# Turning the down-projection of a gated feed-forward block: seven transposed products per pair of f tiles

## The chip, the cores and the metric

The kernel runs on one core of a Trainium2 chip. The metric is the device time in microseconds (us). "TensorE" or PE is the matrix engine, DVE the vector engine, ACT the scalar engine, POOL is GpSimd, and SP is the engine that issues nearly all DMAs here.

## What is computed

One transformer block with adaptive layer norm on 2048 rows of 512 elements: attention with 32 query heads and 8 key-value heads over the last 512 cached positions, and a gated feed-forward block of width 1792, both in float32.

```python
mod = (silu(c) @ w_mod).reshape(c.shape[0], 6, 1, -1)
sa, ca, ga, sb, cb, gb = (mod[:, i] for i in range(6))
h = layernorm(x) * (1 + ca) + sa
x = x + ga * attention(h, k_cache, v_cache, wq, wo)
h = layernorm(x) * (1 + cb) + sb
x = x + gb * ((gelu(h @ w_gate) * (h @ w_up)) @ w_down)
```

## The kernel before

**Numbers.** Every float32 operand of a matmul is kept as two float16 tiles, a high and a low part, and a product is three matmuls (`mm3`): high by high, high by low, low by high. ACT or POOL makes a high part, DVE or POOL the low part by subtraction.

**Stages.** Attention runs first, in 512 steps (`T`) whose order on all engines is written out by hand. In its second half, from step `T // 2 + 30` on, the feed-forward weights are scaled, split and stored to DRAM (`prep_set` for gate and up, `prep_wd` for down), mostly on POOL; the products of the first gate and up sets end attention's last steps. Then comes the feed-forward part. There only SP's queue keeps its written order; on the other engines a planner in the compiler orders the instructions, by written order as priority and by assumed durations.

**The feed-forward part.** The 2048 rows are done in two halves of 1024 (two blocks of 512 columns of the transposed activations). In each half the 14 f tiles of 128 are taken in 7 pairs, so there are 14 pair steps `n`; `n % 7` is the pair, `n // 7` the half. A pair step has two sets, `q = 2n` (gate) and `q = 2n + 1` (up), 28 in all. A set is a 2x2 block product done as seven products instead of eight (the scheme with combined operands t1 to t4 and s1 to s4, `PROD`, `CHAIN`), in the order `ORDER = (1, 2, 6, 7, 5, 4, 3)`; each of the seven steps has 6 matmuls of 512 columns. Partial sums are read in the middle of a chain: the copies after products 1, 6 and 7 are the parts that later sums share. Gate results go through gelu into `G`; up results are multiplied in, and the product is split into parts `A[n, key]`, with key "11", "21" (first block of rows; f tile 1, 2) and "12", "22" (second block).

**Down-projection before.** For each pair step there are 8 row tiles of 128 rows. For each, `y_tasks` multiplies the two parts `A` (as the stationary operand) by the down weights (256 rows, 512 columns, moving): two products of three matmuls into a bank `py`, which one DVE operation adds to the row's sum `acc` with a scale. The tasks are queued in `nexty` at the end of set `2n + 1`, and `y_next` takes one after steps 1, 2, 5 and 6 of each set. `acc` has 8 buffers, for the 8 row tiles of a half: they hold the first half's rows of the residual when the feed-forward part starts. At the last pair of a half `f_final` writes the tile to the output and loads the second half's row tile.

**Names that the change touches.** `prep_wd` (weights, with the gate vector of `rows[5]` multiplied into the columns), `d_spread` (its scales), `result` in `f_items` (parts of the product), `place` (where a copy lies), `f_final`, `attn_final` (which loaded the first half's sums), `y_next` and the loop over `q`, `put_off(n, fn)` (does `fn` after `n` further calls of `tick`, one per step).

Of the kernel before, what the change touches and what calls it, by code (L numbers as in the profile page):

```python
# [9 lines left out]

F32 = mybir.dt.float32
F16 = mybir.dt.float16
BF16 = mybir.dt.bfloat16
AF = mybir.ActivationFunctionType
ALU = mybir.AluOpType
# [23 lines left out]
GU = 2.0 ** -38  # L39
PRE = 2.0 ** -20  # L40
TINY = 1e-36
NOT = 10
LDGAP = 1
NRAW = 5
NRW = 2
GW = 3
NACC = 5
NP16 = 4
# [13 lines left out]
def block_kernel(ctx: ExitStack, tc: tile.TileContext, x, kT, v, wq, wo, wg, wu, wd, cT, wc, wm, out):  # L62
# [14 lines left out]
    def pair(tag, name, bufs):  # L77
        return pool.tile([P, 2, 512], F16, tag=tag, name=name, bufs=bufs)

# [89 lines left out]

    for name, n in (("kmax", HKV), ("kinv", HKV), ("vmax", HKV), ("vsc", HKV), ("wsc", HQ // 2), ("qsc", HQ // 2),  # L170
                    ("ksc", HQ // 2), ("osc", HKV), ("ysc", HKV), ("fsc", NF), ("finv", NF), ("gsc", NF // 2),
                    ("dsc", NF // 2), ("dysc", NF // 2), ("ma", 1), ("mf", 1), ("gam", 2)):
        stats(name, n)

    def col(name, i=0):
        return ST[name][:, i:i + 1]
# [58 lines left out]
    def pool_ts(out, src, a, b=1.0, op0=ALU.mult, op1=ALU.mult):  # L235
        nc.gpsimd.tensor_scalar(out, src, a, b, op0=op0, op1=op1)
# [39 lines left out]
    def o_spread(qd, m, more):  # L276
# [10 lines left out]

        then(second)

    def f_spread(i, m):  # L290
        w = little("lw", 1, 2)
        norm2(w, m, 2, 1.0 / TOP13)
        pool_ts(col("finv", i), w, col("mf"))
        then(lambda: nc.vector.reciprocal(col("fsc", i), w))
        if i % 2 == 0:
            g = col("gsc", i // 2)
            pool_ts(g, col("finv", i), 1.0 / GU)
            then(lambda: nc.vector.reciprocal(g, g))

    def d_spread(n, m, more):  # L300
        w, t = little("lw", 1, 2), little("lt", 1, 2)
        norm2(w, m, 2, 1.0)
        pool_ts(w, w, col("gam", 1), 1.0 / TOP14)
        pool_ts(w, w, 1e-30, 1.0, ALU.max)
        pool_ts(t, col("finv", 2 * n), 2.0 ** 19, col("finv", 2 * n + 1))
        pool_ts(col("dysc", n), t, 2.0 ** 19, w)

        def second():
            nc.vector.reciprocal(col("dsc", n), w)
            more()  # L310

        then(second)
# [289 lines left out]
    def get_wo():  # L602
        return pair("wo", "wo", 8)
# [118 lines left out]
    def at(key, *fns):  # L722
        later.setdefault(key, []).extend(fns)
# [225 lines left out]
    def attn_final(ti):  # L949
        y1[ti] = dram.tile([P, D], F32, name=f"y{ti}")  # L950
        dma(y1[ti], acc[ti])
        nxt = (ti + 2 * QT) % NT
        if ti < 2 * QT:
            own, steps = ln_tile(2, ti, lambda: acc[ti])
# [301 lines left out]
    def f_items(q, hold=None):  # L1256
        n, m = divmod(q, 2)
        st = {}
        done = set()

        def add(k, src):
            nc.vector.tensor_tensor(st[k], st[k], st[src], op=ALU.add)

        def gelu(key, src):

            def apply():
                dst = tmp("fg") if key == "21" else src
                nc.scalar.activation(dst, src, AF.Gelu_apprx_tanh, scale=col("finv", f_scale(q)))
                G[n, key] = dst

            return (apply,)

        def result(key, src):
            if m == 0:
                for step in gelu(key, src):
                    step()
            else:
                g = G.pop((n, key))
                nc.vector.scalar_tensor_tensor(g, g, col("gsc", n % NP), src, op0=ALU.mult, op1=ALU.mult)  # L1279
                t = pair("ot", "at", NOT)  # L1280
                nc.scalar.activation(t[:, 0, :], g, AF.Copy)  # L1281
                nc.vector.tensor_tensor(t[:, 1, :], g, t[:, 0, :], op=ALU.subtract)
# [83 lines left out]

    def prep_wd(n, b):
        m, st = {}, {}
        outs = [staged() for _ in range(2)]

        def load(k):
            st[k] = raw("raw")
            dma(st[k], wd[(2 * n + k) * P:(2 * n + k + 1) * P, :])

        def stat(k):
            if not m:
                m["m"] = little("lm", 4, dtype=BF16)
            sumsq(m["m"][:, k:k + 1], st[k])

        def more():  # L1380
            m["g"] = pool.tile([P, D], F32, tag="gs", name="gs", bufs=1)
            pool_ts(m["g"], rows[5], col("dsc", n))

        def spread():
            d_spread(n, m["m"], more)

        def make(k):
            nc.gpsimd.tensor_tensor(st[k], st[k], m["g"], op=ALU.mult)
            halves(outs[k][0]["t"], st[k])

        sched(b, (lambda: load(0), [lambda: stat(0), nop]), b + 7)
        sched(b + 1, (lambda: load(1), [lambda: stat(1), spread, nop]), b + 4, b + 9)
        for k in range(2):
            sched(b + 7 + 2 * k, (outs[k][1], [lambda k=k: make(k), lambda k=k: store(("wd", n, k), outs[k][0]["t"], 0)]), b + 10 + 2 * k)

    at(T // 2 + 34, lambda: mod_row(5))
    for n in range(NP):
# [1 line left out]
        prep_set(2 * n, b)  # L1399
        prep_set(2 * n + 1, b + 13)  # L1400
        prep_wd(n, b + 21)
    for k in range(2):
        at(T - 1 + 2 * k, lambda k=k: WO.update({("f", 0, k): fetch(("wd", 0, k), get_wo())}))
# [4 lines left out]
    pending = {"raw": [], "rw": []}  # L1408
    loads.sort(key=lambda l: l[0])
    released = {"raw": [0] * NRAW, "rw": [0] * NRW}  # L1410
    for pos, (load, steps), kind, ahead in loads:
        assert len(pos) == len(steps), (pos, len(steps))
        go = pos[0] - ahead
# [140 lines left out]
        at(("f", q, k), *fns)  # L1554

    for n in range(1, 2 * NP):
        for k in range(2):
            f_at(2 * n + 1, 2 * k, lambda n=n, k=k: WO.update({("f", n, k): fetch(("wd", n % NP, k), get_wo())}))
    for q in range(3, NQ):
        for k, at_ in ((0, 2), (3, 2), (1, 3), (2, 4)):  # L1560
            f_at(q - 1, at_, lambda q=q, k=k: set_fetch(("f", q), ("f", q % (2 * NP)), k))
# [18 lines left out]
                step(q + 2 * off, fn)  # L1580

    def f_final(ti):
        if ti >= 2 * QT:
            dma(rows_of(out, ti), acc[ti])
        else:
            put_off(2, lambda: dma(rows_of(out, ti), acc[ti]))
            put_off(5, lambda: load_acc(ti + 2 * QT, y1[ti + 2 * QT]))

    f_done = {(0, k) for k in ORDER} | {(1, 1), (1, 2), (1, 6)}
    for q in range(NQ):  # L1590
        n, m = divmod(q, 2)
        its = items(NG + q) if q < 2 else f_items(q)
        for k, pk in enumerate(ORDER):
            if (q, pk) not in f_done:
                all_of(its[pk])
            run(("f", q, k))
            tick()
            if k in ((1, 2, 5, 6) if q < NQ - 1 else (1, 5)):
# [45 lines left out]
```

## Time and profile before

| | |
|---|---|
| median of 3 runs | 1746.63 us (1746.54 to 1746.77) |
| the profiled execution | 1747.24 us |
| its span, first to last instruction | 1745.3 us |
| TensorE busy | 1723.9 us, 99% of the span, 8080 matmuls |
| DVE, ACT, POOL busy | 79%, 70%, 52% |
| granted TensorE clock | 1.000 |

The span is a little shorter than the execution's time, which also holds what lies before the first and after the last instruction. A row of a group reads: line, engine, operation, output and input tiles, shapes, count, then busy time and the mean of one in ns, then the engine's idle time just before these instructions and what ended it. Rows of the timeline give the start and the duration in us. The duration of a single matmul in such a row contains the pipeline's depth; matmuls start one behind the other at a shorter distance.

### The profile page before, as it was taken

To read this page: it belongs to the slowest core of one execution; us is meant where nothing else is said; L and a number is where in the kernel's file an instruction comes from. 1 tells how busy PE (TensorE), PEld (TensorE's weight loads), DVE (VectorE), ACT (ScalarE), POOL (GpSimd) and SP (SyncE) were. 2 spreads that over 40 slices of the span, in tenths; PEclk is the share of its full clock that TensorE was granted. 3 is DMA by queue.
4 is the path that set the end of the run, shared out by engine and by line. 5 is a ranking of instruction groups with operands and counts; after the bars stand their busy time and mean duration, and the time that the engine had idled before them with its cause. 6 is when DMAs were issued, how large, how long until landed. Compare 5 with 4: busy or idle time off the path is not lost.

```text
span 1745.3 us, 25819 instructions
## 1 busy us (share of the span) xinstructions
PE 1723.9 (99%) x8080; PEld 793.2 (45%) x8082; DVE 1380.3 (79%) x2404; ACT 1213.7 (70%) x2751; POOL 901.1 (52%) x1120
## 2 busy tenths in 40 slices
PE   7999999999999999999999999999999999999999
PEld 5444444444444444444444444444444444444444
DVE  7898898888889999888888888888886655555555
ACT  6988788888879777888777777877784544323232
POOL 4889778776788884654475565554521224000000
PEclk9999999999999999999999999999999999999999
DMA  7999999999999999999999999999986753252222
GB/s 234 219 206 211 211 215 206 225 209 219 213 219 228 212 205 183 212 208 235 212 201 215 203 220 199 211 214 213 195 184 145 205 174 117 81 183 77 88 75 76
DMA packets 667498, 329.71 MB, mean 189 GB/s; under 512 B 561504, under 2 KB 580192, under 8 KB 667360
## 3 DMA queue, kind: packets, MB, share of 16 engines
q1 hardware_dynamic: 667072, 327.54, 82.0%
q8 instruction: 64, 1.05, 0.3%
q14 instruction: 74, 0.61, 0.1%
q10 hardware_dynamic: 288, 0.52, 0.1%
HBM read 131.73 MB, written 59.90 MB: 110 GB/s over the span
## 4 chain that ended last, share of the span: by engine, by line
PE 87%; DVE 4%; ACT 4%; issue 1%; DMA 1%; POOL 1%; SPq 0%; ACTq 0%; POOLq 0%; DVEq 0%
PE py L87 25%; PE po L87 17%; PE ps L87 16%; PE fa L87 8%; PE qa L87 8%; PE fc L87 4%; PE qc L87 4%; PE qb L87 2%; PE fb L87 2%; ACT ee L983 1%; DVE p L1000 1%; ACT p L995 1%; DVE nm L974 1%; DMA pt<-p 1%; PE pq L87 1%
## 5 line engine op out<-in xcount | busy, mean ns | idle before, releaser
L983 ACT ACTIVATE ee<-ps,nm 128x512 f32<-128x512 f32 x512 | 350.2, 684 | 199.2 <-DVE nm L974 196.5
L1000 DVE SCALAR_TENSOR_TENSOR p<-ee,rr,p 128x512 f16<-128x512 f32 x512 | 460.7, 900 | 5.1 <-ACT p L995 4.7
L974 DVE TENSOR_REDUCE nm<-ps 128x1 f32<-128x512 f32 x512 | 350.3, 684 | 111.5 <-PE ps L87 108.4
L87 PE MATMUL ps<-k,qt 128*128 128x512 f16 x1536 | 414.9, 379 | 5.4 <-ACT ee L983 4.2
L87 PE MATMUL po<-pt,v 128*128 128x512 f16 x1536 | 373.0, 379 | 2.0 <-DMA pt<-p 2.0
L995 ACT ACTIVATE p<-ee,rr 128x512 f16<-128x512 f32 x512 | 364.4, 712 | 13.1 <-DVE rr L991 8.8
L87 PE MATMUL py<-wo,ot 128*128 128x512 f16 x1536 | 371.5, 379 | 0.0
L87 PEld LDWEIGHTS <-w 128*128 128x128 f16 x2184 | 213.5, 98 | 258.1 <-DVE w L1045 0.6
L87 PEld LDWEIGHTS <-v 128*128 128x128 f16 x1536 | 149.9, 98 | 184.3 <-DMA pt<-p 2.5
L87 PEld LDWEIGHTS <-ot 128*128 128x128 f16 x1536 | 150.2, 98 | 181.7 <-DVE ot L731 0.5
L87 PEld LDWEIGHTS <-qt 128*128 128x128 f16 x1536 | 145.9, 98 | 176.7 <-issue 4.3
L87 PE MATMUL py<-wo,at 128*128 128x512 f16 x672 | 160.5, 379 | 0.0
L943 DVE SCALAR_TENSOR_TENSOR acc<-py,dysc,acc 128x512 f32<-128x512 f32 x112 | 81.5, 747 | 51.1 <-PE py L87 51.1
L731 DVE SCALAR_TENSOR_TENSOR ot<-po,ot 128x512 f16<-128x512 f32 x128 | 87.7, 685 | 33.0 <-ACT ot L730 32.2
L87 PEld LDWEIGHTS <-at 128*128 128x128 f16 x672 | 65.7, 98 | 79.3
L983 ACT ACTIVATION_READ_ACCUMULATOR ee<-ps,nm 128x1 f32 x512 | 99.9, 195 | 0.0
L943 DVE SCALAR_TENSOR_TENSOR acc<-py,ysc,acc 128x512 f32<-128x512 f32 x128 | 94.7, 740 | 6.2 <-PE py L87 6.2
L1281 ACT ACTIVATE at<-fg 128x512 f16<-128x512 f32 x56 | 35.2, 628 | 72.2 <-DVE fg L1279 71.9
L87 PE MATMUL qa<-t,w 128*128 128x512 f16 x348 | 84.9, 379 | 0.0
L87 PE MATMUL fa<-t,w 128*128 128x512 f16 x336 | 82.0, 379 | 0.0
L730 ACT ACTIVATE ot<-po 128x512 f16<-128x512 f32 x128 | 73.9, 577 | 5.0 <-PE po L87 5.0
L232 POOL TENSOR_TENSOR lw<-lw,half__86 128x1 f32<-128x1 f32 x37 | 22.1, 598 | 104.6 <-DVE lw L182 104.5
(222 smaller groups left out, 2379.9 us busy)
## 6 DMA issues: line engine op xcount, KB each, us to landing
w<-kept SPq DMA_DIRECT2D x123, 256.0 KB, 3.2
wo<-kept SPq DMA_DIRECT2D x60, 256.0 KB, 3.8
raw<-in_wo SPq DMA_DIRECT2D x56, 256.0 KB, 3.3
kept<-stage SPq DMA_DIRECT2D x56, 256.0 KB, 3.4
kept<-w SPq DMA_DIRECT2D x39, 256.0 KB, 3.4
rw<-in_wq SPq DMA_DIRECT2D x38, 256.0 KB, 3.2
hs<-hf SPq DMA_DIRECT2D x32, 256.0 KB, 2.9
pt<-p SPq DMA_TRANSPOSE x512, 3.5
```

The source lines that it names most:

```text
L87: nc.tensor.matmul(ps, a, b, start=first and n == 0, stop=last and n == 2, skip_group_check=chain)
L232: nc.gpsimd.tensor_tensor(out, out, half_, op=ALU.pow)
L730: nc.scalar.activation(t[:, 0, :], src, AF.Copy, scale=scale)
L731: return lambda: nc.vector.scalar_tensor_tensor(t[:, 1, :], src, scale, t[:, 0, :], op0=ALU.mult, op1=ALU.subtract)
L943: nc.vector.scalar_tensor_tensor(acc[ti], st["p"], by, acc[ti], op0=ALU.mult, op1=ALU.add)
L974: nc.vector.tensor_reduce(nm, E[t]["ps"], axis=AX.X, op=ALU.max, negate=True)
L983: nc.scalar.activation(e, E[t]["ps"], AF.Exp, bias=E[t]["nm"], scale=1.0, accum_out=sm[:, t % 2:t % 2 + 1])
L995: nc.scalar.activation(p16[:, 0, :], E[t]["e"], AF.Copy, scale=E[t]["r"])
L1000: nc.vector.scalar_tensor_tensor(p16[:, 1, :], E[t]["e"], E[t]["r"], p16[:, 0, :], op0=ALU.mult, op1=ALU.subtract)
L1281: nc.scalar.activation(t[:, 0, :], g, AF.Copy)
```

## The change

For six of the seven pairs (`turned(n)`), in both halves, the down-projection is computed transposed: the weights become the stationary operand and the 512 columns of a block the moving one, and the 2x2 block product (two f tiles by two halves of the 512 output columns, two blocks of rows) is done by the same scheme of seven products, once for each of two groups of 128 columns in a half (`yt_tasks`). For that:

- `prep_wd` stores four weight tiles per pair instead of two: the plain and combined blocks. The gate vector is no longer multiplied into the columns; it is now a factor per partition (`dyc`) that DVE applies when it adds a product to the sum.
- `result` keeps the four products of a pair until the last is there; `sums_of` makes the combinations t1, t3, t2, t4 by four subtractions on POOL, and their parts on ACT (high) and POOL (low). Plain parts are made of "11", "21" and "22" only.
- Each product's bank is read by DVE at once (`yt_add`) and added to one of eight transposed sums `yt`, of 128 columns by 512 rows, which use the buffers of `acc`.
- After the sixth pair the sums are turned back: ACT parts the 16-bit halves of the float32 words into two blocks (`split`), a transposing DMA turns them (`turn`), ACT puts the halves together again as rows (`yt_rows`), and POOL adds them to the row tile, which is loaded from DRAM when `yt` gives its buffer free. The seventh pair is done as before, on the row tiles; whichever of the two additions comes second calls the output (`f_final`).
- The fourteen tasks are taken one per step of the sets, the last ones two per step. Four weight tiles are fetched per pair.
- More buffers for parts (`NOT`), own buffers for the down weights' loads (`wr`), one gate copy in the buffers of `k`, a smaller scratch area for descriptors.

```diff
-NOT = 10
+NOT = 12
 LDGAP = 1
 NRAW = 5
 NRW = 2
+NWR = 2
...
+    def turned(n):
+
+        return n % NP < NP - 1
...
-        pool_ts(w, w, col("gam", 1), 1.0 / TOP14)
+        pool_ts(w, w, 1.0 if turned(n) else col("gam", 1), 1.0 / TOP14)
         pool_ts(w, w, 1e-30, 1.0, ALU.max)
         pool_ts(t, col("finv", 2 * n), 2.0 ** 19, col("finv", 2 * n + 1))
         pool_ts(col("dysc", n), t, 2.0 ** 19, w)
+        if turned(n):
+            pool_ts(ST["dyc"][:, KT * n:KT * (n + 1)], cols[:, 5, :], col("dysc", n))
...
-            at(now[0] + 3, lambda: load_acc(nxt, y1[nxt]))
...
-                g = G.pop((n, key))
+                g = G[n, key]
                 nc.vector.scalar_tensor_tensor(g, g, col("gsc", n % NP), src, op0=ALU.mult, op1=ALU.mult)
-                t = pair("ot", "at", NOT)
-                nc.scalar.activation(t[:, 0, :], g, AF.Copy)
-                nc.vector.tensor_tensor(t[:, 1, :], g, t[:, 0, :], op=ALU.subtract)
-                A[n, key] = t
+                if not turned(n):
+                    parts(key, G.pop((n, key)), nc.vector)
+                elif key != "12":
+                    parts(key, g, nc.vector)
+                else:
+                    sums_of()
+
+        def parts(key, g, eng):
+            t = A[n, key] = pair("ot", "at", NOT)
+            nc.scalar.activation(t[:, 0, :], g, AF.Copy)
+            eng.tensor_tensor(t[:, 1, :], g, t[:, 0, :], op=ALU.subtract)
+
+        def sums_of():
+            g = {k: G.pop((n, k)) for k in ("11", "12", "21", "22")}
+            for o, a, b in (("11", "12", "11"), ("12", "22", "12"), ("22", "22", "11"), ("21", "21", "22")):
+                nc.gpsimd.tensor_tensor(g[o], g[a], g[b], op=ALU.subtract)
+                parts({"11": "t1", "12": "t3", "22": "t2", "21": "t4"}[o], g[o], nc.gpsimd)
...
-                return tmp("fg")
+                return pool.tile([P, QB], F32, tag="k", name="fg", bufs=2) if k == 6 else tmp("fg")
...
-        outs = [staged() for _ in range(2)]
+        outs = [staged() for _ in range(4)]
+        l, r = slice(0, 256), slice(256, 512)
 
         def load(k):
-            st[k] = raw("raw")
+            st[k] = pool.tile([P, D], F32, tag="wr", name="wr", bufs=NWR)
             dma(st[k], wd[(2 * n + k) * P:(2 * n + k + 1) * P, :])
 
         def stat(k):
...
             sumsq(m["m"][:, k:k + 1], st[k])
 
         def more():
-            m["g"] = pool.tile([P, D], F32, tag="gs", name="gs", bufs=1)
-            pool_ts(m["g"], rows[5], col("dsc", n))
+            if not turned(n):
+                m["g"] = pool.tile([P, D], F32, tag="gs", name="gs", bufs=1)
+                pool_ts(m["g"], rows[5], col("dsc", n))
 
         def spread():
             d_spread(n, m["m"], more)
...
             nc.gpsimd.tensor_tensor(st[k], st[k], m["g"], op=ALU.mult)
             halves(outs[k][0]["t"], st[k])
 
-        sched(b, (lambda: load(0), [lambda: stat(0), nop]), b + 7)
-        sched(b + 1, (lambda: load(1), [lambda: stat(1), spread, nop]), b + 4, b + 9)
-        for k in range(2):
-            sched(b + 7 + 2 * k, (outs[k][1], [lambda k=k: make(k), lambda k=k: store(("wd", n, k), outs[k][0]["t"], 0)]), b + 10 + 2 * k)
+        def out(k):
+            return outs[k][0]["t"] if k < 3 else outs[k][0]["t"][:, :, l]
+
+        def keep_it(k):
+            return lambda: store(("wd", n, k), out(k), 0)
+
+        def tt(o, a, c, op):
+            nc.gpsimd.tensor_tensor(o, a, c, op=op)
+
+        def d0():
+            times(st[0], col("dsc", n))
+            times(st[1], col("dsc", n))
+            halves(out(0)[:, :, l], st[0][:, l])
+            halves(out(0)[:, :, r], st[1][:, l])
+
+        def d1():
+            halves(out(3), st[1][:, r])
+            tt(st[1][:, r], st[0][:, r], st[1][:, r], ALU.add)
+            tt(st[0][:, r], st[0][:, l], st[0][:, r], ALU.subtract)
+
+        def d2():
+            tt(st[0][:, l], st[1][:, r], st[0][:, l], ALU.subtract)
+            tt(st[1][:, l], st[1][:, l], st[0][:, l], ALU.subtract)
+
+        if not turned(n):
+            sched(b, (lambda: load(0), [lambda: stat(0), nop]), b + 7, kind="wr")
+            sched(b + 1, (lambda: load(1), [lambda: stat(1), spread, nop]), b + 4, b + 9, kind="wr")
+            for k in range(2):
+                sched(b + 7 + 2 * k, (outs[k][1], [lambda k=k: make(k), keep_it(k)]), b + 10 + 2 * k)
+            return
+        sched(b, (lambda: load(0), [lambda: stat(0), nop]), b + 10, kind="wr")
+        sched(b + 1, (lambda: load(1), [lambda: stat(1), spread, d2, nop]), b + 4, b + 9, b + 11, kind="wr")
+        sched(b + 7, (outs[0][1], [d0, keep_it(0)]), b + 10)
+        sched(b + 8, (outs[3][1], [d1, keep_it(3)]), b + 11)
+        sched(b + 10, (outs[1][1], [lambda: halves(out(1), st[0]), keep_it(1)]), b + 13)
+        sched(b + 11, (outs[2][1], [lambda: halves(out(2), st[1]), keep_it(2)]), b + 14)
...
+    def wd_fetch(n, k):
+        t = get_wo()
+        WO["f", n, k] = fetch(("wd", n % NP, k), t if k < 3 else t[:, :, 0:256])
+
+    for k, pos in zip((0, 3, 2, 1), (T - 1, T + 1, T + 3, T + 6)):
+        at(pos, lambda k=k: wd_fetch(0, k))
...
-        for k in range(2):
-            f_at(2 * n + 1, 2 * k, lambda n=n, k=k: WO.update({("f", n, k): fetch(("wd", n % NP, k), get_wo())}))
+        for k, at_ in ((0, 1), (2, 3), (1, 4), (3, 5)) if turned(n) else ((0, 1), (1, 4)):
+            f_at(2 * n + 1, at_, lambda n=n, k=k: wd_fetch(n, k))
...
+        assert ti in back
+        if ti not in halfway:
+            return halfway.add(ti)
         if ti >= 2 * QT:
             dma(rows_of(out, ti), acc[ti])
         else:
             put_off(2, lambda: dma(rows_of(out, ti), acc[ti]))
-            put_off(5, lambda: load_acc(ti + 2 * QT, y1[ti + 2 * QT]))
+
+    YT, YR, back, halfway = {}, {}, set(), set()
+
+    def yt_add(n, c, qb, ps):
+        by = ST["dyc"][:, KT * (n % NP) + c:KT * (n % NP) + c + 1]
+        key = (n // NP, c, qb)
+        if key in YT:
+            nc.vector.scalar_tensor_tensor(YT[key], ps, by, YT[key], op0=ALU.mult, op1=ALU.add)
+        else:
+            YT[key] = pool.tile([P, QB], F32, tag="acc", name="yt", bufs=2 * QT)
+            nc.vector.tensor_scalar(YT[key], ps, by, None, op0=ALU.mult)
+
+    def yt_turn(g, c, qb):
+
+        def split():
+            u = YR["u", c, qb] = pool.tile([P, 2, QB], U16, tag="p16", name="yu", bufs=NP16)
+            nc.scalar.activation(u, YT[g, c, qb].bitcast(U16).rearrange("p (r h) -> p h r", h=2), AF.Copy)
+
+        def turn():
+            if ("t", qb) not in YR:
+                YR["t", qb] = pool.tile([P, KT, 2 * QT, P], U16, tag="pt", name="yv", bufs=NPT)
+            nc.sync.dma_start_transpose(YR["t", qb][:, c], YR.pop(("u", c, qb)).rearrange("p a b -> p (a b)"))
+
+        split()
+        put_off(2, turn)
+        YR["n"] = YR.get("n", 0) + 1
+        if YR["n"] % QT == 0:
+            for i in range(QT):
+                ti = 2 * QT * g + (YR["n"] - 1) % (2 * QT) // QT * QT + i
+                put_off(3, lambda ti=ti: load_acc(ti, y1[ti]) or back.add(ti))
+
+    def yt_rows(g, qb):
+        t = YR.pop(("t", qb)).rearrange("p c (h i) q -> p c q h i", h=2)
+        for i in range(QT):
+            ti = 2 * QT * g + QT * qb + i
+            assert ti in back
+            r = raw("yr")
+            nc.scalar.activation(r.bitcast(U16).rearrange("p (c q h) -> p c q h", c=KT, h=2), t[:, :, :, :, i], AF.Copy)
+            nc.gpsimd.tensor_tensor(acc[ti], acc[ti], r, op=ALU.add)
+            f_final(ti)
+
+    ADDS = {1: ((0, 0),), 2: ((0, 0),), 6: ((0, 1),), 5: ((1, 1),), 7: ((1, 1),), 4: ((1, 0),), 3: ((0, 1),)}
+    YORDER = (1, 2, 6, 5, 7, 3, 4)
+    LAST = {2: (0, 0), 7: (1, 1), 3: (0, 1), 4: (1, 0)}
+
+    def yt_tasks(n):
+        tasks = []
+        for p in range(2):
+            st = {}
+            bk = banks(st, {"a": ("acc", "ya", NACC) if p else ("qa", "ya", 1), "b": ("acc", "yb", NACC), "c": ("acc", "yc", NACC)})
+
+            def group(k, p=p, bk=bk):
+                a, b = PROD[k]
+                x, start = CHAIN[k]
+                ci, off = YCOL[a]
+                w, t = WO["f", n, ci], A[n, {"b11": "11", "b21": "21", "b22": "22"}.get(b, b)]
+                sl = slice(off + p * P, off + (p + 1) * P)
+                mm3(bk(x)(), w[:, 0, sl], w[:, 1, sl], t[:, 0, :], t[:, 1, :], start, k in (2, 4, 3), True)
+
+            def post(k, p=p, st=st):
+                (i, qb), = ADDS[k]
+                yt_add(n, 2 * i + p, qb, st[CHAIN[k][0]])
+                if n % NP == NP - 2 and k in LAST:
+                    i, qb = LAST[k]
+                    c, g = 2 * i + p, n // NP
+                    put_off(1, lambda: yt_turn(g, c, qb))
+                    if p and k in (3, 4):
+                        put_off(7 if g else 9, lambda: yt_rows(g, qb))
+
+            tasks += [[(lambda k=k, f=group: f(k), lambda k=k, f=post: f(k))] for k in YORDER]
+        return tasks
+
+    YCOL = {"a11": (0, 0), "a12": (0, 256), "s2": (1, 0), "s3": (1, 256), "s4": (2, 0), "s1": (2, 256), "a22": (3, 0)}
...
+            if n and k == 2 and m == 0 and turned(n - 1):
+                nexty += yt_tasks(n - 1)
+            if k in ((1, 2, 5, 6) if q < NQ - 1 else (1, 5)) or (n and turned(n - 1)):
                 y_next()
-        if m == 1:
+            if q == NQ - 2 and k > 1 or (q, k) in ((NQ - 1, 1), (NQ - 1, 2)):
+                y_next()
+        if m == 1 and not turned(n):
             for qi, (a, b) in enumerate((("11", "21"), ("12", "22"))):
                 for i in range(QT):
...
-                                         [("f", n, 0), ("f", n, 1)], col("dysc", n % NP), f_final if n % NP == NP - 1 else None))
+                                         [("f", n, 0), ("f", n, 1)], col("dysc", n % NP), f_final))
     while nexty:
         y_next()
+        tick()
...
-    nc = _bacc.Bacc("TRN2", target_bir_lowering=False, num_devices=1)
+    nc = _bacc.Bacc("TRN2", target_bir_lowering=False, num_devices=1, dynamic_dma_scratch_size=1024)
```

More of the change, by code (lines that the diff above doesn't have):

```diff
@@ L12 @@
 F16 = mybir.dt.float16
+U16 = mybir.dt.uint16
 BF16 = mybir.dt.bfloat16
@@ L171, in block_kernel @@
                     ("ksc", HQ // 2), ("osc", HKV), ("ysc", HKV), ("fsc", NF), ("finv", NF), ("gsc", NF // 2),
-                    ("dsc", NF // 2), ("dysc", NF // 2), ("ma", 1), ("mf", 1), ("gam", 2)):
+                    ("dsc", NF // 2), ("dysc", NF // 2), ("dyc", KT * NF // 2), ("ma", 1), ("mf", 1), ("gam", 2)):
         stats(name, n)
@@ L951, in attn_final @@
         dma(y1[ti], acc[ti])
-        nxt = (ti + 2 * QT) % NT
         if ti < 2 * QT:
+            nxt = ti + 2 * QT
             own, steps = ln_tile(2, ti, lambda: acc[ti])
@@ L1406, in block_kernel @@
             at(pos, lambda q=q, k=k: set_fetch(("f", q), ("f", q), k))
-    pending = {"raw": [], "rw": []}
+    pending = {"raw": [], "rw": [], "wr": []}
     loads.sort(key=lambda l: l[0])
-    released = {"raw": [0] * NRAW, "rw": [0] * NRW}
+    released = {"raw": [0] * NRAW, "rw": [0] * NRW, "wr": [0] * NWR}
     for pos, (load, steps), kind, ahead in loads:
@@ L1556, in block_kernel @@
     for n in range(1, 2 * NP):
-        for k in range(2):
-            f_at(2 * n + 1, 2 * k, lambda n=n, k=k: WO.update({("f", n, k): fetch(("wd", n % NP, k), get_wo())}))
+        for k, at_ in ((0, 1), (2, 3), (1, 4), (3, 5)) if turned(n) else ((0, 1), (1, 4)):
+            f_at(2 * n + 1, at_, lambda n=n, k=k: wd_fetch(n, k))
     for q in range(3, NQ):
@@ L1597, in block_kernel @@
             tick()
-            if k in ((1, 2, 5, 6) if q < NQ - 1 else (1, 5)):
+            if n and k == 2 and m == 0 and turned(n - 1):
+                nexty += yt_tasks(n - 1)
+            if k in ((1, 2, 5, 6) if q < NQ - 1 else (1, 5)) or (n and turned(n - 1)):
                 y_next()
-        if m == 1:
+            if q == NQ - 2 and k > 1 or (q, k) in ((NQ - 1, 1), (NQ - 1, 2)):
+                y_next()
+        if m == 1 and not turned(n):
             for qi, (a, b) in enumerate((("11", "21"), ("12", "22"))):
```

1 line of the change is left out of this document (removed).

## Prediction

> **What bounds the kernel now.** I read the page first (share of each engine), then busy time by stretches, then what TensorE waits for, then the chain's end.
>
> ```profile
> span 1745.3 us, 25819 instructions
> ...
> PE 1723.9 (99%) x8080; PEld 793.2 (45%) x8082; DVE 1380.3 (79%) x2404; ACT 1213.7 (70%) x2751; POOL 901.1 (52%) x1120
> ```
> ```profile
> 830.00:1100.00 270.00, 270.00 (x1263) 122.59 (x1262) 225.91 (x397) 212.54 (x500) 148.99 (x192) 1.00 0.96 209
> ...
> 1340.00:1500.00 160.00, 159.46 (x740) 72.17 (x738) 95.78 (x146) 66.88 (x108) 44.85 (x51) 1.00 0.50 152
> ...
> 1500.00:1746.00 246.00, 241.51 (x1119) 109.31 (x1117) 132.49 (x193) 72.85 (x116) 0.00 (x0) 1.00 0.30 98
> ```
> ```profile
> PE fa L87 <- ACT fg L876: 0.5, 1, 0.5
> ```
> ```profile
> 1732.44 9.08 PE py L87 x42
> 1741.52 0.03 issue
> 1741.55 0.75 DVE acc L943
> ```
>
> The columns of the middle fence are length, then busy time of PE, weight load, DVE, ACT, POOL, then granted clock, DMA share, GB/s. TensorE is busy without a break both while the weights are prepared (830 to 1100) and in the feed-forward part (1340 to the end); there it waited once, 0.5 us, at a granted clock of 1.00. So the feed-forward part takes as long as its matmuls take, 9.08 / 42 = 0.216 us each. DVE is at 54% there, ACT at 30%, POOL idle after 1500. After the last matmul come an add (0.75 us) and the output's way out.
>
> **What is removed.**
>
> ```profile
> L87 PE MATMUL py<-wo,at 128*128 128x512 f16 x672 | 160.5, 379 | 0.0
> ...
> L943 DVE SCALAR_TENSOR_TENSOR acc<-py,dysc,acc 128x512 f32<-128x512 f32 x112 | 81.5, 747 | 51.1 <-PE py L87 51.1
> ...
> L1282 DVE TENSOR_TENSOR at<-fg,at 128x512 f16<-128x512 f32 x55 | 39.6, 721 | 14.7 <-ACT at L1281 13.6
> ...
> L1281 ACT ACTIVATE at<-fg 128x512 f16<-128x512 f32 x55 | 34.6, 628 | 70.3 <-DVE fg L1279 70.1
> ```
>
> A pair's down-projection is 8 row tiles x 2 sources x 3 terms = 48 matmuls; 14 of these make the 672. Turned, it is 2 column halves x 7 products x 3 = 42, of the same 512 columns. Twelve of the 14 are turned: 72 fewer, 72 x 0.216 = **15.55 us** off TensorE. Since nothing else ends last in this stage, all of it leaves the path, unless something new makes TensorE wait.
>
> **What is added in the feed-forward part.** A turned pair now fills 126 x 0.216 = 27.2 us of TensorE instead of 28.5. DVE adds 14 partial sums instead of 8 and makes one low part less: 0.54 x 28.5 + 6 x 0.747 - 0.72 = 19.2 us, 70%. ACT makes 7 high parts instead of 4: 0.30 x 28.5 + 3 x 0.63 = 10.3 us, 38%. POOL gets four subtractions and four low parts. The nearest rows are the same shapes in the feed-forward part, where POOL makes combinations (minimum / median / maximum ns):
>
> ```profile
> L565 POOL TENSOR_TENSOR cb<-cb x8: 1262/1269/1726, 1432.1 to 1470.3; 128x512 f32<-128x512 f32 x8
> ...
> L369 POOL TENSOR_TENSOR t<-cb,t x8: 1153/1160/1606, 1437.3 to 1472.7; 128x512 f16<-128x512 f32 x8
> ```
>
> 4 x (1.27 + 1.16) = 9.7 us, 36%. No engine becomes full. The question is latency: t1 to t4 can only be made when the last product (3) of the pair's second set is in, and product 6 of the down-projection, the third in its order, needs t2. Written order puts between them the rest of that step (3 matmuls), four steps of 9, and product 6 of the next set (6): 45 matmuls, and t2's low part is read by the third term, so 47 x 0.216 = 10.15 us. How fast the way there is, the last set of the trace shows:
>
> ```profile
> 1724.94 1.46 PE L87 MATMUL fa<-t,w 128*128 128x512 f16 x6
> ...
> 1726.43 0.60 ACT L876 ACTIVATE u<-fa 128x512 f32<-128x512 f32 x1 [1.15 <-PE fa L87]
> ...
> 1730.98 1.46 PE L87 MATMUL fc<-b,w 128*128 128x512 f16 x6
> ...
> 1732.48 0.69 DVE L1262 TENSOR_TENSOR u<-u,fc 128x512 f32<-128x512 f32 x1 [0.55 <-PE fc L87]
> ...
> 1733.69 0.75 DVE L1279 SCALAR_TENSOR_TENSOR fg<-fg,gsc,u 128x512 f32<-128x512 f32 x1
> ```
>
> Product 3 ends at 1732.44; the add and the scaling take 0.69 + 0.75, so "12" is there after 1.4 us (the trace has a low part between them). Then POOL. If the planner lets subtractions go ahead while ACT makes high parts (0.63), t2's low part is the seventh operation: 4 x 1.27 + 3 x 1.16 = 8.6, ready at 10.0. Strictly in turn it is 3 x (1.27 + 0.7 + 1.16) = 9.4, ready at 10.8. Against 10.15 that is from 0.1 early to 0.7 late, per pair. TensorE's order here is laid out by the planner from assumed durations, so lateness is hidden only if the planner expected it. The trace speaks a little against that:
>
> ```profile
> 1434.86 1.46 PE L87 MATMUL fa<-t,x 128*128 128x512 f16 x6
> ...
> 1435.58 1.73 POOL L565 TENSOR_TENSOR cb<-cb 128x512 f32<-128x512 f32 x1
> ...
> 1436.87 0.98 DVE L1282 TENSOR_TENSOR at<-fg,at 128x512 f16<-128x512 f32 x1
> ...
> 1437.34 0.63 ACT L365 ACTIVATE t<-cb 128x512 f16<-128x512 f32 x1 [0.50 <-POOL cb L565]
> ...
> 1440.13 0.63 ACT L365 ACTIVATE t<-cb 128x512 f16<-128x512 f32 x1 [2.17 <-POOL cb L565]
> 1440.67 0.67 ACT L1268 ACTIVATE fg<-fa,finv 128x512 f32<-128x512 f32 x1
> ```
>
> ACT stood 2.17 us behind POOL at 1440, while the gelu next in its queue had its input since the matmuls that ended at 1436.3: the plan took POOL to be faster than it is. I take 0.3 us per pair, between 0 and 0.7: **+3.6 us** (0 to 8.4).
>
> Where POOL and a DVE operation on SBUF alone overlap, both stretch (POOL 1.73 for 1.27, DVE 0.98 for 0.69). The Trainium skill (SBUF — State Buffer, "SBUF: two separate sides") says that the pair of ports which VectorE and GpSimd share is an exclusive lock, the loser blocked for the whole instruction; the stretched pair agrees in direction, and by that rule the chain could be longer, which is the second rival below. The skill's GPSIMD Engine Reference ("Engine selection") advises against elementwise work with two inputs on GpSimd as about twice as slow as VectorE; the rows here, 1.27 against 0.69, agree, and moving it to DVE would shorten the chain.
>
> **The other edges.** Turning back: 16 splits and 16 row assemblies of 1024 16-bit elements on ACT, 16 transposing DMAs, 16 adds on POOL.
>
> ```profile
> L511 ACT ACTIVATE b<-hf 128x256 f16<-128x256 f32 x24 | 9.1, 416 | 0.0
> ```
> ```profile
> DMA to landing us min/median/max: 3.1/3.8/5.2
> ```
> ```profile
> SPq L93 <- PE fa L87: 217.7, 28, 16.3
> ```
>
> From 256 to 512 elements ACT goes from 0.416 to 0.628, so 1024 cost about 1.05 us (an estimate), 34 us over both halves of the rows, on an engine at 38%. The middle line is the transpose of layer-norm tiles in this stage. SP's queue, which the transposes, reloads of sums and the now four weight fetches a pair share in written order, spends its time waiting for weight buffers (last line), so it has room; a transpose is written two steps after its split, and blocks nothing if ACT is on time. Between the halves, DVE's first sums of the second half wait for output tiles to leave their shared buffers: 0 to 2 us, once, and POOL is shared with the layer-norm combinations for two pairs of the first half; I take +1 together.
>
> The end: after the last product, 8 tiles x 6 matmuls = 10.4 us remain, then the add. The last transposed sums' way: product 4 ends some 5.2 us before that point, add 0.75, split 1.05, transpose 3.8 (lands at about +0.5 to 1.4), then ACT has eight assemblies of 1.05 and two high parts, about +8.6 to 9.9, and POOL adds 1.27. That is 9.9 to 11.2 against 11.2 for the matmul path: nearly level. DVE's add of one tile stands behind POOL's, so I take +1 (0 to 2).
>
> **The preparation**, 830 to 1290, beside attention:
>
> ```profile
> L1335 POOL TENSOR_TENSOR rw<-rw 128x256 f32<-128x256 f32 x56 | 48.0, 857 | 4.4
> ...
> L156 POOL TENSOR_TENSOR stage<-rw,stage 128x512 f16<-128x512 f32 x42 | 54.7, 1303 | 3.5
> ...
> L155 POOL TENSOR_SCALAR stage<-rw 128x512 f16<-128x512 f32 x42 | 31.2, 743 | 17.0 <-DMA kept<-stage 14.5
> ...
> L159 POOL TENSOR_SCALAR rw<-rw,fsc 128x512 f32<-128x512 f32 x28 | 22.9, 818 | 71.0 <-ACT p L995 40.0 <-ACT ee L983 30.0 <-DVE fsc L294 1.0
> ...
> L1388 POOL TENSOR_TENSOR raw<-raw,gs 128x512 f32<-128x512 f32 x14 | 19.5, 1396 | 0.6
> ...
> L156 POOL TENSOR_TENSOR stage<-rw,stage 128x256 f16<-128x256 f32 x14 | 9.8, 699 | 1.2
> ...
> L155 POOL TENSOR_SCALAR stage<-rw 128x256 f16<-128x256 f32 x14 | 7.7, 553 | 1.2
> ...
> L236 POOL TENSOR_SCALAR gs<-gate,dsc 128x512 f32<-128x512 f32 x7 | 4.8, 693 | 17.3 <-DVE dsc L309 11.1 <-ACT p L995 4.0 <-ACT ee L983 2.0
> ```
>
> Before, per pair: 0.69 + 2 x (1.40 + 0.74 + 1.30) = 7.6 us. After: 2 x 0.82 + 2 x (0.74 + 1.30) + 3 x (0.55 + 0.70) + 4 x 0.86 = 12.9. That is +5.3 a pair, 32 in all, on an engine that was at 55%. TensorE does not wait for it: the results are needed hundreds of microseconds later. Two more stores a pair go behind the transposes in SP's queue. I take 0; bounds: nothing can be gained where TensorE never waited, and up to 5 if POOL's extra load slows DVE (84% busy) enough to delay attention.
>
> **Sum** against the profiled execution's 1747.2 (0.6 above the median): -15.55 + 3.6 + 1 + 1 = -9.95, so 1737.3, or 1736.7 on the median's footing.
>
> **The rivals.**
> 1. *The copies inside the gate and up chain.* Between product 6 and 7 of a set ACT must copy the bank. It ends 0.03 + 0.60 us after product 6; 6 down-projection matmuls (1.3 us) covered it, 3 (0.65 us) barely do. With 0.2 us handoff uncovered in 24 sets it is +4.8: 1741.5. Against it: the planner already mixes other products between.
> 2. *POOL's chain decides, slower.* If the six operations up to t2 collide with DVE (1.73 and 1.61 rather than 1.27 and 1.16) about every other time and the planner didn't expect it, t2 comes 2 us late, 12 times: +24 in place of 3.6, so 1757. It decides from 1.3 us per pair, where 15.55 is used up. For it: the ACT wait above. Against it: DVE's operations on SBUF alone become fewer in a turned pair.
> 3. *Attention or the end gives it back*: preparation +5, the end and the change of halves +5 rather than 2, chain as forecast: 1744.7.
> That the matmuls don't go is no open question: they are counted in the code.
>
> **Chances.** Forecast (about 1731 to 1741) 0.55; rival 1 0.15, of which about half stays faster by over 0.2% (3.5 us, about what a measurement of this kernel can tell from no change); rival 2 0.18, slower; rival 3 0.12, a third faster, half level, the rest slower. Faster 0.55 + 0.08 + 0.04 = 0.67, same 0.07 + 0.06 = 0.13, slower 0.20. The range starts at the saving with no loss, 1746.6 - 15.6 = 1731, less half a microsecond, and reaches to 1750, into rival 2, whose worst half is left out.
>
> **What would show it.** Right: 600 matmuls py in place of 672 (named ya, yb, yc in part), TensorE still without gaps from 1340 on, waits of TensorE for POOL or ACT's t-parts under 5 us in all, the last matmul some 10 us earlier and the end the same 3 us behind it. Wrong: a row of TensorE waits for t tiles, once per turned pair, over a microsecond each; or the chain ending in POOL's row adds; or TensorE gaps before 1340.

## The result and the profile after

| | median | ratio to the kernel before, 95% interval |
|---|---|---|
| before | 1746.70 us | |
| after | 1754.85 us | 1.0045 (1.0027 to 1.0062) |

The change made the kernel slower by 8 us (0.45%); 1736.7 was forecast, and the range ended at 1750. The profiled execution's span went from 1745.3 to 1754.4, +9.1. The same views as before, first the page, then the stretches (length, busy PE, weight load, DVE, ACT, POOL, granted clock, DMA share, GB/s), then the chain's end:

```profile
span 1754.4 us, 26202 instructions
...
PE 1713.0 (98%) x8008; PEld 785.4 (45%) x8010; DVE 1424.3 (81%) x2464; ACT 1263.0 (72%) x2819; POOL 1069.8 (61%) x1292
```
```profile
830.00:1100.00 270.00, 269.93 (x1263) 122.21 (x1261) 225.19 (x398) 212.47 (x498) 169.40 (x231) 1.00 0.99 214
1340.00:1500.00 160.00, 156.97 (x724) 70.50 (x723) 119.12 (x171) 76.25 (x128) 94.03 (x91) 1.00 0.50 152
1500.00:1700.00 200.00, 198.06 (x918) 89.45 (x917) 131.33 (x191) 88.78 (x135) 68.51 (x56) 1.00 0.43 128
1700.00:1755.00 55.00, 36.15 (x152) 14.92 (x149) 25.43 (x37) 25.28 (x31) 19.74 (x16) 0.90 0.49 132
```
```profile
1734.17 4.34 ACT yr L1685 x4
1738.52 0.53 ACT at L1296
1739.05 0.05 issue
1739.09 7.73 PE py L89 x24
1746.83 0.03 issue
...
1747.27 0.75 DVE acc L951
```

The 72 matmuls went, as counted (8080 to 8008). But TensorE, which had one wait of 0.5 us from 1340 on before, is idle for 5 us between 1340 and 1700, and busy for only 36 of the last 55 us; and the chain that ended last, which was matmuls up to the final add, now leads through row assemblies (yr) on ACT. TensorE's six largest waits from 1340 on, with their total, times and longest:

```profile
PE py L89 <- ACT at L1296: 5.3, 2, 4.8
PE fa L89 <- ACT u L884: 2.2, 1, 2.2
PE fa L89 <- DMA w<-kept: 1.9, 1, 1.9
PE fa L89 <- ACT fu L884: 1.9, 1, 1.9
PE fa L89 <- ACT fg L884: 1.5, 1, 1.5
PE ya L89 <- ACT at L1296: 0.9, 2, 0.6
```

All but the third end in ACT. The last 50 us, from the timeline:

```profile
1702.88 0.75 DVE L1655 SCALAR_TENSOR_TENSOR yt<-yb,dyc,yt 128x512 f32<-128x512 f32 x1 [1.19 <-PE yb L89]
...
1704.29 1.04 ACT L1664 ACTIVATE yu<-yt 128x1024 uint16<-128x1024 uint16 x1
...
1706.52 0.75 DVE L1655 SCALAR_TENSOR_TENSOR yt<-yb,dyc,yt 128x512 f32<-128x512 f32 x1
...
1715.14 1.40 DVE L1655 SCALAR_TENSOR_TENSOR yt<-yc,dyc,yt 128x512 f32<-128x512 f32 x2
...
1717.23 2.95 ACT L1664 ACTIVATE yu<-yt 128x1024 uint16<-128x1024 uint16 x3 [2.57 <-DVE yt L1655]
...
1718.19 1.41 DVE L1655 SCALAR_TENSOR_TENSOR yt<-ya,dyc,yt 128x512 f32<-128x512 f32 x2 [0.33 <-PE ya L89]
...
1720.71 1.46 PE L89 MATMUL fa<-t,w 128*128 128x512 f16 x6 [1.91 <-ACT fu L884]
...
1721.60 1.06 ACT L1664 ACTIVATE yu<-yt 128x1024 uint16<-128x1024 uint16 x1 [0.94 <-DMA yv<-yu]
...
1724.42 1.46 PE L89 MATMUL fa<-t,w 128*128 128x512 f16 x6 [2.25 <-ACT u L884]
...
1727.34 4.75 SPq L1669 DMA_TRANSPOSE yv<-yu  x3
...
1732.14 2.00 SPq L95 DMA_DIRECT2D acc<-y  x4
...
1733.10 5.42 ACT L1685 ACTIVATE yr<-yv 128x1024 uint16<-128x1024 uint16 x5 [1.62 <-DMA yv<-yu]
...
1735.73 10.28 POOL L1686 TENSOR_TENSOR acc<-acc,yr 128x512 f32<-128x512 f32 x8 [25.09 <-DMA acc<-y]
1738.42 0.61 ACT L1296 ACTIVATE at<-fg 128x512 f16<-128x512 f32 x1
...
1739.09 7.72 PE L89 MATMUL py<-wo,at 128*128 128x512 f16 x24 [4.80 <-ACT at L1296]
1742.37 8.73 SPq L95 DMA_DIRECT2D out_y<-acc  x8
```

Product 2 alone fills the banks yb. Its two adds, which complete the first two of the eight sums, end at 1703.6 and 1707.3; the last adds of the other six end between 1715.9 and 1719.6. One split (yu) had run at 1704.3. The other seven, with that of the second sum among them, come from 1717.2 on, after ACT had stood idle for 2.57 us until the sum of the first of them was complete. The copies (fu, u) that the last set's chain waits for stand behind them in ACT's queue: 1.9 and 2.25 us. A split also waits for a buffer of an earlier transpose. SP issues the last transposes up to 1732 and reloads row tiles behind them. Then five assemblies stand ahead of the last high part (at), whose input had been there since 1733.0: 4.8 us. After that wait 24 matmuls take 7.72 us, not 24 x 0.216 + 0.16 = 5.3. And the last rows leave 7.6 us after the last matmul instead of 3.8, since five output writes are issued together at the end.

The account of the +9.1: -15.5 for the matmuls; +1.0 before the feed-forward part; +4.4 for waits up to 1545 (4.9, less the 0.5 of before); +10.7 for waits after 1700; +2.4 slow matmuls; +3.8 the way out. Of the remaining 2.3, about 2.0 belongs to the waits as well: a wait is listed from the end of the matmul before it, and a matmul lasts 0.379 - 0.216 = 0.16 us longer than the distance to the next, so each wait costs that much more, thirteen times instead of once.

### The profile page after: what moved, and what is told of

It is laid out like the page before. It is cut to its first block, busy times and chain, and to the rows that moved or that the text cites. A ratio compares the mean times of both kernels' runs of the same rounds, so it can differ in the third digit from the quotient of the medians.

```text
span 1754.4 us, 26202 instructions
## 1 busy us (share of the span) xinstructions
PE 1713.0 (98%) x8008; PEld 785.4 (45%) x8010; DVE 1424.3 (81%) x2464; ACT 1263.0 (72%) x2819; POOL 1069.8 (61%) x1292
## 4 chain that ended last, share of the span: by engine, by line
PE 81%; DVE 5%; ACT 5%; DMA 3%; POOL 3%; issue 2%; SPq 0%; DVEq 0%; POOLq 0%; ACTq 0%
PE py L89 18%; PE po L89 16%; PE ps L89 16%; PE qa L89 8%; PE fa L89 6%; PE qc L89 4%; PE fc L89 3%; PE ya L89 2%; PE qb L89 2%; PE fb L89 2%; PE yc L89 1%; DMA pt<-p 1%; ACT ee L990 1%; ACT p L1002 1%; PE pq L89 1%
## 5 line engine op out<-in xcount | busy, mean ns | idle before, releaser
L1302 POOL TENSOR_TENSOR fg<-fg 128x512 f32<-128x512 f32 x48 | 62.3, 1299 | 142.4 <-DVE fg L1286 141.4
L1296 ACT ACTIVATE at<-fg 128x512 f16<-128x512 f32 x92 | 56.9, 625 | 66.8 <-DVE fg L1286 40.0
L396 POOL TENSOR_TENSOR rs<-rs,nhalf 128x1 f32<-128x1 f32 x32 | 18.7, 584 | 102.6 <-DVE rs L390 99.7
L1655 DVE SCALAR_TENSOR_TENSOR yt<-ya,dyc,yt 128x512 f32<-128x512 f32 x84 | 61.8, 745 | 23.9 <-PE ya L89 23.5
L89 PE MATMUL ya<-at,wo 128*128 128x512 f16 x288 | 77.5, 379 | 1.5 <-ACT at L1296 0.9
```

What stands on the lines that cost most here:

```text
L89: nc.tensor.matmul(ps, a, b, start=first and n == 0, stop=last and n == 2, skip_group_check=chain)
L396: nc.gpsimd.tensor_tensor(st["rs"], st["rs"], nhalf, op=ALU.pow)
L1302: nc.gpsimd.tensor_tensor(g[o], g[a], g[b], op=ALU.subtract)
L1655: nc.vector.scalar_tensor_tensor(YT[key], ps, by, YT[key], op0=ALU.mult, op1=ALU.add)
```

## The experiments

Theory A: the turning back at the end holds up the queues, and TensorE with them. Theory B, the second rival of the prediction: POOL's chain to t1 to t4 is late in every turned pair. The diffs are against the changed kernel; "..." stands for lines left out.

**e1: no turning back in the second half.**

```diff
-        split()
-        put_off(2, turn)
+        if g == 0:
+            split()
+            put_off(2, turn)
...
     def yt_rows(g, qb):
+        if g:
+            for i in range(QT):
+                f_final(2 * QT * g + QT * qb + i)
+            return
```

> Leaves out, in the second half of the rows only, the turning back: no splits and no row assemblies on ACT, no transposing DMAs, no row adds on POOL (so the second half's output lacks the six turned pairs). Everything else, the turned products included, stays. Theory A (the turning back at the end holds up ACT's queue, and TensorE with it): the stalls of 1.9, 2.25 and 4.8 us, the slow matmuls behind the last of them (2.5 us) and the longer way out after the last matmul (3.8 us) go, 15.3 us together: 1739.6. Theory B (my rival of POOL's chain: t1 to t4 come late, and the last pair shows it most): the stalls stay, 1750 or more.

Measured: 1738.32 us, ratio 0.9951 (0.9936 to 0.9966). After 1545 no wait of TensorE is listed. The second half's way back costs 1754.85 - 1738.32 = 16.5 us, and theory A's price for it was 15.3. Theory B's 1750 is out by far.

**e2: five pairs turned in place of six.**

```diff
-        return n % NP < NP - 1
+        return n % NP < NP - 2
...
-                        put_off(7 if g else 9, lambda: yt_rows(g, qb))
+                        put_off(9, lambda: yt_rows(g, qb))
```

The second change puts the second half's assemblies two steps later; also, in the last two sets one task at most is taken per step, not two.

> Five of seven pairs are turned instead of six, in both halves, so that two plain pairs stand behind the last turned one and cover the turning back; the output is the reference's. Theory A: 12 matmuls more (2.6 us), 15.3 us of the end back: 1742.2. Theory B (a loss with every turned pair: 15.55 us saved and 24.7 lost over twelve): ten twelfths of both, 1746.7 - 13 + 20.6 = 1754.

Measured: 1748.72 us, ratio 1.0010 (1.0001 to 1.0019). Better by 6 us with 12 more matmuls, but 6.5 short of theory A's figure. In its trace the way back, in the same queues, holds up other things:

```profile
1717.55 1.47 PE L89 MATMUL fc<-t,w 128*128 128x512 f16 x6 [0.90 <-DMA w<-kept]
...
1722.40 1.46 PE L89 MATMUL fa<-t,w 128*128 128x512 f16 x6 [0.79 <-ACT fu L884]
...
1726.12 2.76 PE L89 MATMUL py<-wo,at 128*128 128x512 f16 x12 [2.26 <-DVE acc L951]
```

weights behind transposes on SP, a copy behind assemblies on ACT, banks kept by DVE, whose row adds stand behind POOL's. More cover alone isn't enough.

**e3: ACT in written order in the last two sets.**

```diff
+        if q == NQ - 2:
+            ctx.enter_context(tc.manual_schedule(engines={mybir.EngineType.SP, mybir.EngineType.Activation}))
```

> In the last two sets ACT keeps the written order instead of the planner's; nothing else is changed. If it is the order that the planner gave ACT (row assemblies ahead of the last high part, splits ahead of the copies between products), the 4.8 us stall and the 2.5 us of slow matmuls behind it go, 1747.5, and down to 1743.5 if the copies come free as well. If it is the amount of work on ACT at the end, it stays at 1752 or more.

Measured: 1754.98 us, ratio 1.0043 (1.0028 to 1.0058): no change. The expectation's second branch came out, but not quite for its reason. The 4.8 us wait is gone, and TensorE ends at 1740 instead of 1746.8; the time went into the other end of the same work, since the assemblies now come last, POOL's adds end at 1744.8, and by the medians the kernel ends where it did:

```profile
1733.32 8.61 ACT L1685 ACTIVATE yr<-yv 128x1024 uint16<-128x1024 uint16 x8
1734.55 10.29 POOL L1686 TENSOR_TENSOR acc<-acc,yr 128x512 f32<-128x512 f32 x8 [24.26 <-ACT yr L1685]
```

So ACT's order alone is not at fault: in either order the way back takes some 26 us from the last sum (1719) to the last row add, longer than the work that stands beside it.

**e4: the combinations on DVE instead of POOL** (`sums_of`: `nc.gpsimd` to `nc.vector`, twice).

> The four subtractions and the four low parts of t1 to t4 are made by DVE instead of POOL in every turned pair. Theory B: the chain to t2 becomes shorter by some 7 x 0.55 us and TensorE's waits for it vanish: if they were the main loss, below 1747. Theory A: only the 2.7 us of stalls at t parts and at POOL's queue before 1700 can go, and DVE gets 5.5 us more per pair: 1752 to 1757.

Measured: 1759.48 us, ratio 1.0066 (1.0049 to 1.0083). Slower still by 4.6 us, and 2.5 above the range that theory A gave. DVE is 88% busy between 1340 and 1500 (141.22 of 160). TensorE waits there 2.6 us for a high part and 2.5 us for a bank that DVE had not yet read, and at 1547 2.1 us for weights:

```profile
1546.77 2.55 PE L89 MATMUL fa<-b,w 128*128 128x512 f16 x6 [2.08 <-DMA w<-kept]
```

After these three waits 29 matmuls in all follow at half pace, 6 us lost. With DVE this full, POOL was the better place. Nothing came back as theory B would have it; after e1 this is the second result against it.

**e5: no turning back in either half** (as e1, for both).

> Leaves out the turning back in both halves of the rows (splits, transposing DMAs, row assemblies, row adds), so the output lacks the six turned pairs. It gives what the turned products alone are worth. If the 1.9 us wait for gate weights (1539 in the changed kernel's trace) comes from the first half's transposes ahead of the weights in SP's queue, it goes: 1738.3 - 1.8 = 1736.5. If that wait has another source: 1738.

Measured: 1735.89 us, ratio 0.9939 (0.9924 to 0.9953). The first half's way back costs 2.4 us, and the wait near 1539 is gone with it. What the turned products are worth by themselves is 10.9 us of the 15.55; TensorE's waits in this trace still come to 3.8 us, all before 1460, where the kernel before had 0.5.

**e6: the first half's way back written later**, with buffers of its own for the splits; the reloads and assemblies move as well.

```diff
-            u = YR["u", c, qb] = pool.tile([P, 2, QB], U16, tag="p16", name="yu", bufs=NP16)
+            tag, bufs = ("p16", NP16) if g else (("qt", 3), ("v16", 2))[YR.get("s", 0) % 5 > 2]
...
-        put_off(2, turn)
+        put_off(2 if g else 6, turn)
...
-                put_off(3, lambda ti=ti: load_acc(ti, y1[ti]) or back.add(ti))
+                put_off(3 if g else 5, lambda ti=ti: load_acc(ti, y1[ti]) or back.add(ti))
...
-                        put_off(7 if g else 9, lambda: yt_rows(g, qb))
+                        put_off(7 if g else 12, lambda: yt_rows(g, qb))
```

> The changed kernel with the first half's transposing DMAs written six steps behind their splits instead of two, the reloads two steps and the row assemblies three steps later, and the splits in buffers of their own (those of the queries and values, free by then); the second half as in the changed kernel. If SP's queue standing before the transposes is what makes the gate weights late, the 1.9 us stall near 1539 goes: 1753. The end stays as it was, since nothing of it is changed. If it is not the queue: 1754.9.

Measured: 1749.65 us, ratio 1.0016 (1.0006 to 1.0026). The wait at 1539 is gone, so it came from what stood ahead of the weights in SP's queue, the transposes and reloads. It gained 5.2 us, though, not 1.9: the planner laid out the end in another way too, where I had expected no difference. There TensorE still waits 1.8, 0.9 and 7.0 us for ACT. By the two traces, the other 3 us are in the main 1.2 us less of other waits, six fewer waits at 0.16 us each, and a way out of 6.4 us after the last matmul instead of 7.6; why the planner's new order has these effects stays open.

**e7: five pairs, and the way back later in both halves**, with no plain task between the products after the second step of the last set but one, and the splits in buffers of their own.

```diff
-        return n % NP < NP - 1
+        return n % NP < NP - 2
...
-        put_off(2, turn)
+        put_off(6, turn)
...
-                put_off(3, lambda ti=ti: load_acc(ti, y1[ti]) or back.add(ti))
+                put_off(7, lambda ti=ti: load_acc(ti, y1[ti]) or back.add(ti))
...
-                        put_off(7 if g else 9, lambda: yt_rows(g, qb))
+                        put_off(14, lambda: yt_rows(g, qb))
```

> Five of seven pairs turned as in e2, and in both halves the way back is written later: transposes six steps behind the splits, reloads seven, row assemblies fourteen; splits in buffers of their own; in the last two sets no plain task is taken between the products, so that sixteen of them (20.7 us of matmuls) stand behind the last product. The output is the reference's. If what remained in e2 (0.9 + 0.8 + 2.3 + 0.7 us at the end, 1.8 us between the halves) is the way back standing before weights, copies and sums in the queues of SP, ACT and DVE, it goes: 1748.7 - 6.5 = 1742.2, and with it the kernel is faster than before. If the way back costs its time wherever it stands: 1748.

Measured: 1744.21 us, ratio 0.9986 (0.9977 to 0.9995): faster than before by 2.6 us, 2 us short of the expectation. At the end two waits of 1.7 and 1.6 us for ACT are left, the first behind three splits.

**e8: e7 with the splits on POOL.**

```diff
-            nc.scalar.activation(u, YT[g, c, qb].bitcast(U16).rearrange("p (r h) -> p h r", h=2), AF.Copy)
+            nc.gpsimd.tensor_copy(u, YT[g, c, qb].bitcast(U16).rearrange("p (r h) -> p h r", h=2))
```

> As e7, but the sixteen splits of the 16-bit halves are made by POOL instead of ACT. In e7 TensorE still waited 1.7 and 1.6 us for ACT copies that stood behind three splits. If ACT's queue is what is left, these go: 1744.2 - 3.3 = 1741. If POOL's splits are so slow that the way back becomes the end's path, or hold up the parts of t1 to t4: 1746 or more.

Measured: 1740.86 us, ratio 0.9961 (0.9947 to 0.9975), as expected. Both waits are gone, and after 1460 none is listed.

**e9: e6 (six pairs), with the second half's splits on POOL** and in the buffers that e6 gave the first half's.

> Six pairs turned as in e6, with the second half's splits on POOL and in the buffers of e6's first half. TensorE's two waits for copies behind splits (1.8 and 0.9 us in e6) should go, and the third one (7.0 us, the last high part behind row assemblies, with slower matmuls after it) depends on when the transposes land. If the way back is simply longer than the work that covers it (about 18 us), the end comes no earlier than 1747, whatever engine splits; if ACT's splits were the cause, 1740.

Measured: 1752.77 us, ratio 1.0031 (1.0020 to 1.0043). That is 3 us slower than e6. The waits behind splits went here too, but the chain's end leads through POOL's row adds, as in e3, and the last pair's weights now come late behind the transposes in SP's queue:

```profile
1729.55 9.82 PE L89 MATMUL py<-wo,at 128*128 128x512 f16 x33 [3.56 <-DMA wo<-kept]
```

What helped with two plain pairs behind the way back doesn't help with one.

**e10: e6, with the second half turned back by TensorE.**

```diff
...
+    def yt_back(ti):
+        qb, i = divmod(ti - 2 * QT, QT)
+        ps = bank("acc", "pb", NACC)
+        for c in range(KT):
+            nc.tensor.transpose(ps[:, c * P:(c + 1) * P], YT[1, c, qb][:, i * P:(i + 1) * P], ident)
+        nc.vector.tensor_tensor(acc[ti], acc[ti], ps, op=ALU.add)
+        f_final(ti)
...
```

> Six pairs turned as in e6 (first half turned back by DMA, written later); in the second half the sums are turned back by TensorE: 32 transposes of 128x128 against the identity into banks of partial sums, added to the row tiles by DVE, placed between the last set's products; no splits, transposing DMAs, assemblies or POOL adds there, and the row tiles are loaded early into buffers that are free. The output is the reference's. Four such transposes took 0.44 us in attention (at 699.6 in the trace before), so 32 cost 3.5 us. If the end's loss is the length and the queues of the way back, it is replaced by that: 1738.3 (e1) - 1.8 (the weights' wait) + 3.5 = 1740.0, faster than before by 0.4%. If the turned products themselves or the last parts keep the end late: 1746.

Measured: 1740.56 us, ratio 0.9962 (0.9950 to 0.9974), 0.6 from the expectation. The end, as the chain and the timeline show it:

```profile
1721.59 2.45 PE pb L1704 x16
1724.04 10.47 PE py L89 x48
1734.52 0.03 issue
1734.54 0.75 DVE acc L951
```

The matmuls run to the last add again, one wait of 0.5 us aside. e8 and e10 beat the kernel before by 6.3 and 6.6 us, and the changed kernel by 14.

## Why the prediction was wrong

- **The saving** (-15.55): right; 72 matmuls fewer at 0.216 us.
- **POOL's chain** (+3.6, 0 to 8.4; rival 2 with 0.18): within its range, and not the loss. TensorE's waits for parts are 0.3, 0.6 and 0.25 us up to 1704, a third of what I took. The subtractions and low parts on POOL took 1.30 and 1.21 us against the 1.27 and 1.16 of the sum:

```profile
L1302 POOL TENSOR_TENSOR fg<-fg 128x512 f32<-128x512 f32 x48 | 62.3, 1299 | 142.4 <-DVE fg L1286 141.4
...
L1297 POOL TENSOR_TENSOR at<-fg,at 128x512 f16<-128x512 f32 x48 | 57.4, 1206 | 0.0
```

- **Between the halves and the combinations** (+1): too small, 2.4 us by e5 against e1, and 1.5 us more for a copy behind a layer-norm part that waits for POOL at 1459. Costing SP's queue at nothing was wrong: "blocks nothing if ACT is on time" held for neither half, as e6 showed for the first. From 1340 on SP waited for splits eight times, 33.1 us in all, the longest time for 12.5 us after 1705:

```profile
SPq L1669 <- ACT yu L1664: 33.1, 8, 12.5
```

- **The end** (+1, 0 to 2): this is the step that failed, by 15 us; e1 measured 16.5. The durations in it were near: splits 1.05, transposes 3.4 to landing, adds 1.29, and assemblies 1.16 where I had 1.05. What was wrong is that I followed the last sum alone up to its landing and let the other seven be on their way already. Six of them come within 4 us, and at 1717 seven splits were still to be made; so seven splits, seven transposes, eight reloads, eight assemblies and eight adds pass one after the other through ACT, SP, ACT again and POOL. From the end of the last product 4 (1718.8) to the last row add (1746.0) they take 27 us, where my sum has 15.1 to 16.4 (5.2, and then 9.9 to 11.2). And I gave the way back no effect on what it shares queues with; the last set's copies and parts, on ACT, are on TensorE's path. A slip in the sum is small beside this: 8 x 1.05 + 2 x 0.63 = 9.7 after a landing at +0.5 to 1.4 gives 10.2 to 11.1, not 8.6 to 9.9.
- **The preparation** (0 to 5): TensorE began the feed-forward part 1.0 us later in this profile; in the experiments it was 0.1 earlier to 1.3 later. Small, as taken, with POOL's added 20 us between 830 and 1100 visible.
- **The rivals**: the third, "the end gives it back", named the right place at 5 us, a third of the price. The copy between products 6 and 7 (rival 1) never appears as a wait in the changed kernel before the end (the 1.5 us at 1459 are for the copy after product 7); there it does, with 2.25 us, but because of the splits.

## What to carry to other kernels

Work that is taken off the bound engine and handed to four others is not hidden because each of them has room on average: where a stage ends, the whole chain counts, with all its items, against the work that is really left beside it. Compare the two lengths before choosing the path. At such an end a detour through DMA and three queues can cost more than doing the thing on the bound engine itself: in e10, 32 transposes on TensorE took some 4 us, with eight adds on DVE, in place of a way back that cost 16.5.

## What the runs showed of the hardware

Four float32 transposes of 128x128 on TensorE take 0.44 us (in attention, in the kernel before) to 0.61 us together (2.45 us for sixteen in e10), and POOL (in e8) copies 1024 16-bit elements per partition as fast as ACT (in the changed kernel), by the middle figure, the median:

```profile
L1666 POOL COPY yu<-yt x16: 1035/1041/1512, 1487.8 to 1700.5; 128x1024 uint16<-128x1024 uint16 x16
```
```profile
L1664 ACT ACTIVATE yu<-yt x16: 1039/1050/1057, 1507.4 to 1725.7; 128x1024 uint16<-128x1024 uint16 x16
```

Matmuls ran at half pace after some waits, 0.43 us apart instead of 0.216, at a granted clock of 0.50 to 0.54 in these stretches. In the changed kernel, after 4.80 us, 24 of them took 2.4 us too long; in e3 six took 2.72 us instead of 1.46 after a wait of 2.52 us; in e4 7, 14 and 8 were slow after waits of 2.56, 2.52 and 2.08 us. After 2.25 us (in the changed kernel) and 2.26 us (in e2) they ran at full speed, so the length of the last wait alone does not decide. The Trainium skill (TensorE: Matmul & The Clock Gate, "What's actually happening") says that TensorE's clock falls to half after an idle window of some 3.4 us, by windows that run freely. The slow matmuls agree in their pace but not in that length: the 2.08 us in e4 were enough, with no other listed wait in the 80 us before.
